# A retention layer and an MLP on one core: scores and sums of a head pair in one block of products, and a new order of the first units

## The chip, the cores and the metric

The kernel runs on one core of a Trainium2 chip. The time is the device time of one execution in microseconds (us); the kernel before took 1026.29 us (median of 3 runs, 1025.18 to 1026.33). Lower is better. "Faster" and "slower" mean a change of more than 2%.

The engines of the core work side by side, each through its own instructions in order: TensorE (PE in the profile, PEld for its weight loads) multiplies matrices and writes them to PSUM; VectorE (DVE), ScalarE (ACT) and GpSimd (POOL) work element by element; SyncE (SP) starts most of the transfers (DMA). An engine waits on semaphores where it needs another engine's result, or a buffer that another still reads.

## The reference

Per batch and head (8 batches, 8 heads, 576 positions, 64 features), a retention layer: causal scores with a decay that depends on the distance, times the values. Then an MLP with a PReLU over all 8 x 576 = 4608 tokens.

```python
# q, k, v: (8, 8, 576, 64)
scores = 64 ** -0.5 * np.matmul(q, k.transpose(0, 1, 3, 2))
gamma  = 1.0 - 2.0 ** (-5.0 - np.arange(8))
rel    = pos[:, None] - pos[None, :]
Dmat   = np.where(rel >= 0, gamma[:, None, None] ** rel, 0.0)
x      = np.matmul(scores * Dmat, v)            # -> (4608, 512): tokens x (head, feature)
h      = x @ w_in                               # w_in (512, 2048), 64-bit floats in memory
g      = np.maximum(h, 0) + alpha * np.minimum(h, 0)
out    = g @ w_out                              # w_out (2048, 512)
```

## The kernel before

Names used below. A *pair* n is two heads of one batch: 32 pairs, 4 to a batch. Its 576 positions are 9 chunks of 64. Within a chunk the kernel takes masked *scores* (tile `ps`, then `mt`); over the chunks it keeps *running sums* of k^T v (products in tile `pu`, sums in `su`, copied into `vn`); the *values* (`pv`) are then one product per chunk and head of [sums; v] with [q; scores], and land in x^T (`xb`). A *block* kb is 256 tokens; there are 18. A *unit* (kb, i) is one eighth of the MLP of a block. Blocks 0 and 1 are done in the plain way while the weights arrive and are converted; from block 2 on, both products of the MLP are done by a 7-product scheme (7 products of half-size matrices instead of 8), so a unit is 14 products `ph` of 128 columns, then sums on VectorE to `g`, then 7 products `po` of 256 columns. In the trace each f32 product shows as two matmul records.

One unit, and the sums at the end of a block:

```python
    def mlp_unit(kb, i):                       # ps_h has one buffer for each tag
        ph = [ps_h.tile([P, 4, P], FP32, tag=f"psh{m}") for m in range(2)]
        for n, (m, o, l, r) in enumerate((...)):          # 7 products, 2 parts each
            for cc in range(2):
                nc.tensor.matmul(ph[m][:, o], w_in[...], r[:, cc], ...)
        g = mlp.tile([P, 8, P], FP32, tag="g")
        nc.scalar.copy(g[:, 7], ph[0][:, 2])
        for o, x0, x1 in (...):                           # 4 sums that read ph (3 of 128x256)
            nc.vector.tensor_tensor(out=o, in0=x0, in1=x1, op=ALU.add)
        for m in range(2):
            nc.vector.tensor_scalar(g[...], g[...], 0.0, alpha[...], ALU.min, ALU.mult)
        nc.vector.scalar_tensor_tensor(...)               # max(x, 0) + the above, 128x512
        for o, x0, x1, op in (...):                       # 4 sums, 128x128
            ins = nc.vector.tensor_tensor(...)
        pend.append((kb, i, g))
        if len(pend) > 1:
            mlp_out()                          # the po of the unit BEFORE this one

    def mlp_out():
        kb, i, g = pend.pop(0)
        if i == 0:
            acc[kb] = [ps_o.tile([P, 2, HM], FP32, tag=f"pso{n}") for n in range(4)]  # 1 buffer
        for n, (x, y) in enumerate(PROD):      # 7 products into po0, po0, po1, po1, po2, po2, po3
            nc.tensor.matmul(acc[kb][n // 2][:, n % 2, :], g[:, x, :], w_out[i][:, y, :], ...)
        if i == NU - 1:
            out_block(kb, acc.pop(kb))

    def out_block(kb, po):                     # end of a block
        nc.scalar.copy(s1, p1)
        for o, x, y, op in (...):              # 6 sums 128x256 that read po0..po2
            nc.vector.tensor_tensor(out=o, in0=x, in1=y, op=op)
        nc.vector.tensor_tensor(out=osb[:, 1, 0], in0=p4, in1=u3, op=ALU.add)  # reads po3
```

A later pair (ps_a has two buffers for all its tiles, one PSUM bank each), and the loop that deals pairs and units:

```python
    def pair_scores(n, kT, qT):
        ps = [ps_tile([P, NM, C], ...) for p2 in range(2)]
        ...                                    # 9 chunks x 2 heads: 18 products 64x64
        for h2 in range(2):
            nc.scalar.copy(mt[half(h2), h2]..., qT[half(h2)])
        for p2 in range(2):
            for h2 in range(2):                # 4 masks, 64x320 and 64x256
                nc.vector.scalar_tensor_tensor(out=mt[...], in0=ps[p2][...], scalar=th[...],
                                               in1=mask[...], ...)
    def pair_states(n, kn, vn):
        ps = [ps_tile([P, NM - 1, D], f"pu{p2}_{n}") for p2 in range(2)]
        ...                                    # 8 chunks x 2 heads: 16 products 64x64
        nc.scalar.copy(su[:, 0::2], ps[0])
        ...                                    # VectorE: 2 of 64x256, 3 of 128x64, 1 of 128x192
    def pair_sums(vn, su):
        for h2 in range(2):
            nc.scalar.copy(vn[half(h2), h2, 1:], su[half(h2)])

    for n, (b, c) in enumerate(pairs):         # from pair 8 on
        ...
        share = -(-len(queue) // (NPAIR - c))  # 4 or 5 units to a pair
        cuts = [(share + i) // 3 for i in range(3)][::-1]
        kT, qT = turned.pop(n)
        mt = pair_scores(n, kT, qT)
        pop_units(cuts[0])
        pair_sums(vn, pair_states(n, kn, vn))
        pop_units(cuts[1])
        ... scale_pair(n + 1); transposes(n + 1)
        pair_values(n, vn, mt)
        pop_units(cuts[2])
```

The first batch is taken in parts of 256 positions, with all heads at once. The pieces of the weights are converted from 64-bit floats by `piece_in` (ScalarE, two operations) and `piece_out` (VectorE, three of 128x512, then one on GpSimd):

```python
    def part_states(x):
        ...                                    # 32 products
        for j in range(4):
            u = banks[j % 2][:, j // 2]
            if was is None:
                nc.scalar.copy(sums[x][j], u)
            else:
                nc.vector.tensor_tensor(out=sums[x][j], in0=was, in1=u, op=ALU.add)
            was = sums[x][j]
    def part_values(x):
        ...
        nc.scalar.copy(to[:, 0], banks[0])     # x^T for the first units
        for h2 in range(2):
            nc.scalar.copy(to[half(h2), 1], banks[1][half(1 - h2)])
    def plain_out(kb, i, g):
        for m in range(2):
            for x in range(2):
                nc.tensor.matmul(acc[kb][m], g[:, 2 * x + m], w_out[i][...], ...)
```

Of the kernel before, what the change touches and what calls it, by code (L numbers as in the profile page):

```python
# [18 lines left out]
def kernel(  # L19
# [54 lines left out]

    IN_FLIGHT = 5 << 18
    flight = []

    def load(to, src, size):
        ins = nc.sync.dma_start(to, src)
        if gated[0]:  # L80
            ahead = size
            for other, n in reversed(flight):
                if ahead >= IN_FLIGHT:
                    tc.add_manual_dep(ins.ins, other.ins.name, mybir.DependencyInfo(
                        mybir.DependencyClass.Sync, mybir.DependencyReason.DATA),
                        reason="bytes in flight")
                    break
                ahead += n
            flight.append((ins, size))

    gated = [True]

# [280 lines left out]

    def mlp_out():
        kb, i, g = pend.pop(0)
        if kb in PLAIN:
            return plain_out(kb, i, g)
        if i == 0:
            acc[kb] = [ps_o.tile([P, 2, HM], FP32, tag=f"pso{n}", name=f"po{n}_{kb}")
                       for n in range(4)]  # L380
        for n, (x, y) in enumerate(PROD):
            nc.tensor.matmul(acc[kb][n // 2][:, n % 2, :], g[:, x, :], w_out[i][:, y, :],  # L382
                             start=(i == 0 and n % 2 == 0),
                             stop=(i == NU - 1 and (n % 2 == 1 or n == 6)),
                             skip_group_check=True)
        if i == NU - 1:
            out_block(kb, acc.pop(kb))

    def plain_out(kb, i, g):
        if i == 0:
            acc[kb] = [ps_o.tile([P, DM], FP32, tag=f"pso{2 * kb + m}", name=f"po{m}_{kb}")
                       for m in range(2)]
        for m in range(2):
            for x in range(2):
                nc.tensor.matmul(acc[kb][m], g[:, 2 * x + m],  # L397
                                 w_out[i][:, 2 * x:2 * x + 2].rearrange("p x f -> p (x f)"),
                                 start=(i == 0 and x == 0), stop=(i == NU - 1 and x == 1))
        if i == NU - 1:  # L400
            po = acc.pop(kb)
            osb = ring.tile([P, 2, DM], FP32, tag=f"o{kb}", name=f"osb_{kb}")
            for m in range(2):
                t0 = kb * TB + m * P
                nc.scalar.copy(osb[:, m], po[m])
                nc.sync.dma_start(out[t0:t0 + P, :], osb[:, m])
        if kb == PLAIN[-1] and i % UST == UST - 1:
            waiting.extend((w_in[i // UST], x) for x in S_WORK)
            waiting.extend((w_out[j], x) for j in range(i + 1 - UST, i + 1) for x in T_WORK)
# [39 lines left out]

    def mlp_unit(kb, i):  # L450
        if kb not in xt:
# [5 lines left out]
        for n, (m, o, l, r) in enumerate((  # L457
# [3 lines left out]
            for cc in range(2):  # L461
                nc.tensor.matmul(ph[m][:, o], w_in[i // UST][:, l, i % UST, cc], r[:, cc],  # L462
                                 start=(n in (0, 3) and cc == 0), stop=(n in (2, 6) and cc == 1),
                                 skip_group_check=True)

# [19 lines left out]
        combine(3, ins)  # L486
        assert i < NU - UST or not waiting
        pend.append((kb, i, g))
        if len(pend) > 1:
# [14 lines left out]

    def pop_units(n):
        for _ in range(min(n, len(queue))):
            kb, i = queue.pop(0)
            mlp_unit(kb, i)
            if i == NU // 2 and kb + 1 < NKB and ready[kb + 1] <= done[0]:
# [54 lines left out]
    def pair_states(n, kn, vn):  # L564
        c = pairs[n][1]
        ps = [ps_tile([P, NM - 1, D], f"pu{p2}_{n}") for p2 in range(2)]
        for j in range(NJ - 1):
            for h2 in range(2):
                x = (h2, 1 - h2)[j % 2]
                nc.tensor.matmul(ps[j % 2][half(x), j // 2], kn[half(1 - h2), j],  # L570
                                 vn[half(1 - h2), h2, j], start=True, stop=True)
        su = attn.tile([P, S], FP32, tag="kT", name=f"su_{n}")[:, 0:S - D].rearrange(
            "p (j d) -> p j d", d=D)
        g1, g2 = gch[:, 0, c:c + 1], gch[:, 1, c:c + 1]
        nc.scalar.copy(su[:, 0::2], ps[0])
        for h2 in range(2):
            nc.vector.scalar_tensor_tensor(
                out=su[half(h2), 1::2], in0=su[half(h2), 0::2], scalar=g1[half(h2)],
                in1=ps[1][half(1 - h2)], op0=ALU.mult, op1=ALU.add)
        for j in range(3, NJ - 1, 2):  # L580
            nc.vector.scalar_tensor_tensor(out=su[:, j], in0=su[:, j - 2], scalar=g2,
                                           in1=su[:, j], op0=ALU.mult, op1=ALU.add)
        nc.vector.scalar_tensor_tensor(out=su[:, 2::2], in0=su[:, 1:NJ - 3:2], scalar=g1,  # L583
                                       in1=ps[0][:, 1:], op0=ALU.mult, op1=ALU.add)
        return su

    def pair_sums(vn, su):
        for h2 in range(2):
            nc.scalar.copy(vn[half(h2), h2, 1:], su[half(h2)])  # L589

    def pair_values(n, vn, mt):
# [80 lines left out]
    def part_states(x):  # L672
# [12 lines left out]
        for j in range(4):  # L685
            u = banks[j % 2][:, j // 2]
            if was is None:
                nc.scalar.copy(sums[x][j], u)
            else:
                nc.vector.tensor_tensor(out=sums[x][j], in0=was, in1=u, op=ALU.add)  # L690
# [6 lines left out]
    def part_values(x):  # L697
# [23 lines left out]
        to = xb[x].rearrange("p c (m q s) -> p q c m s", m=2, q=2)  # L721
        nc.scalar.copy(to[:, 0], banks[0])
        for h2 in range(2):
            nc.scalar.copy(to[half(h2), 1], banks[1][half(1 - h2)])  # L724

# [40 lines left out]
    fetch(6)  # L766
    load_part(1)
    fetch(8)
    load_part(2)
# [3 lines left out]
    part_scale(0, 2)  # L773
    part_scores(0)
    part_states(0)
    piece_in(2)
# [3 lines left out]
    aps = ps_a.tile([P, NFC], FP32, tag="psa", name="aps")  # L780
    nc.tensor.transpose(aps, a16, ident[0:NFC, 0:NFC])
    nc.vector.tensor_copy(alpha, aps)
    nc.vector.tensor_scalar(nalpha, alpha, -1.0, None, ALU.mult)
    piece_in(3)
    piece_out(2)
    part_scale(1, 1)
    piece_in(1)
    plain_unit(0, 0)
# [3 lines left out]
    part_transposes(1, 0)  # L792
    mlp_out()
    part_transposes(1, 1)
    piece_out(1)
    piece_in(1)
    piece_out(1)
    part_scores(1)
    part_states(1)
    part_scale(2, 1)  # L800
    part_scale(2, 2)
    piece_in(1)
    plain_unit(0, 1)
    piece_out(1)
    plain_relu()
    piece_in(1)
    part_values(1)
    part_carry(1)
    last_transposes()
# [17 lines left out]

    gated[0] = False

# [56 lines left out]
    for n, (b, c) in enumerate(pairs):  # L886
# [7 lines left out]
        share = -(-len(queue) // (NPAIR - c))  # L894
        cuts = [(share + i) // 3 for i in range(3)][::-1]
        kT, qT = turned.pop(n)
        mt = pair_scores(n, kT, qT)
        pop_units(cuts[0])
        pair_sums(vn, pair_states(n, kn, vn))
        pop_units(cuts[1])  # L900
        if n + 1 < len(pairs):
            scale_pair(n + 1)
            turned[n + 1] = transposes(n + 1)
        pair_values(n, vn, mt)
        del loaded[n]
        pop_units(cuts[2])
        if c == NPAIR - 1:
# [32 lines left out]
```

## Time and profile before

| | busy, us | share of the span |
|---|---|---|
| TensorE, products (PE) | 1007.9 | 98% |
| TensorE, weight loads (PEld) | 891.0 | 87% |
| VectorE (DVE) | 768.8 | 75% |
| ScalarE (ACT) | 267.5 | 26% |
| GpSimd (POOL) | 176.7 | 17% |

The span of the profiled execution is 1024.7 us. Up to some 160 us the plain units run; from there to the end the 7-product units, with pairs 8 to 31 between them up to some 880 us. A line of the timeline has: start in us, duration in us, engine, line of the kernel, operation, tile written <- tiles read, shapes, count; in brackets, idle time before it and what ended it. A duration there runs to the end of the last instruction and overlaps the next line, so the time that a piece costs its engine is best read from start to start.

### The profile page before, as it was taken

The page shows a single profiled execution, that of the slowest core. Times are in us where ns is not written, and L with a number is a line of the kernel's source. Part 1 is how long each engine was busy: PE and PEld are TensorE (multiplying, and loading weights), DVE is VectorE, ACT ScalarE, POOL GpSimd, SP SyncE. Part 2 cuts the span into 40 slices and gives each one's busy share as a digit, 9 for nine tenths or more (in the row PEclk, how much of TensorE's full clock was granted, in tenths as well). Part 3 has the DMA queues.
Part 4 walks back from the last instruction along what each step waited for, and adds up shares of the span by engine and source line. Part 5 has one row for each costly group of instructions (what it writes and reads, how often), then busy time and mean ns, then how long its engine had stood idle before and what let it go on. Part 6 is the DMA issues. An engine that isn't in the chain of part 4 may idle for free.

```text
span 1024.7 us, 23101 instructions
## 1 busy us (share of the span) xinstructions
PE 1007.9 (98%) x9385; PEld 891.0 (87%) x9385; DVE 768.8 (75%) x2041; ACT 267.5 (26%) x599; POOL 176.7 (17%) x198
## 2 busy tenths in 40 slices
PE   6899999999999999999999999999999999999998
PEld 5666668999999999999999999999999999999997
DVE  7669967777878787776868787877787776667665
ACT  4556652223222222022122222222222211000000
POOL 4656675200200010100010000200020001010000
PEclk9999999999999999999999999999999999999999
DMA  9975744223223222112113222222222100000000
GB/s 237 234 195 146 184 75 97 46 59 59 62 42 67 49 46 57 24 45 45 41 31 67 47 52 46 63 46 59 48 47 57 24 22 2 22 1 21 1 21 22
DMA packets 229308, 64.30 MB, mean 63 GB/s; under 512 B 214337, under 2 KB 222545, under 8 KB 229201
## 3 DMA queue, kind: packets, MB, share of 16 engines
q1 hardware_dynamic: 227088, 62.29, 26.8%
q8 instruction: 74, 1.21, 0.5%
q10 hardware_dynamic: 2112, 0.53, 0.3%
q14 instruction: 34, 0.27, 0.1%
HBM read 53.35 MB, written 9.44 MB: 61 GB/s over the span
## 4 chain that ended last, share of the span: by engine, by line
PE 97%; DVE 1%; DMA 1%; ACT 0%; issue 0%; POOL 0%; ACTq 0%; DVEq 0%; POOLq 0%
PE ph L462 40%; PE po L382 38%; PE po L397 6%; PE ph L418 5%; PE pv L600 3%; PE ps L551 2%; PE pu L570 2%; DMA w_out<-in_q_dram 1%; PE pv L717 0%; PE pv L706 0%; PE ps L660 0%; DVE w_out L690 0%; PE pt L641 0%; DVE wc L308 0%; DVE pa L667 0%
## 5 line engine op out<-in xcount | busy, mean ns | idle before, releaser
L382 PE MATMUL po<-w_out,g 128*128 128x256 f32 x1792 | 407.8, 379 | 0.0
L382 PEld LDWEIGHTS po<-w_out,g 128*128 128x128 f32 x1792 | 331.1, 190 | 39.4
L473 DVE TENSOR_TENSOR g<-ph,g 128x256 f32<-128x256 f32 (+1 forms) x512 | 187.5, 387 | 184.9 <-ACT g L468 112.7
L462 PE MATMUL ph<-xb,w_in 128*128 128x128 f32 x2048 | 277.8, 279 | 0.0
L462 PEld LDWEIGHTS ph<-xb,w_in 128*128 128x128 f32 x2048 | 253.2, 192 | 8.1 <-issue 0.5
L462 PE MATMUL ph<-xt,w_in 128*128 128x128 f32 x1536 | 213.4, 275 | 0.0
L462 PEld LDWEIGHTS ph<-xt,w_in 128*128 128x128 f32 x1536 | 192.1, 192 | 0.0
L468 ACT COPY g<-ph 128x128 f32<-128x128 f32 x128 | 33.9, 265 | 395.7 <-PE ph L462 375.6
L484 DVE TENSOR_TENSOR g<-g 128x128 f32<-128x128 f32 x512 | 126.8, 289 | 7.8
L478 DVE SCALAR_TENSOR_TENSOR g<-g 128x512 f32<-128x512 f32 x128 | 91.7, 717 | 3.9
L476 DVE TENSOR_SCALAR g<-g,alpha 128x256 f32<-128x256 f32 x256 | 85.0, 374 | 3.7
L523 POOL TENSOR_TENSOR qx<-qx,tabx 128x576 f32<-128x576 f32 x28 | 32.7, 1167 | 310.9 <-DMA qx<-in_q_dram 255.0
L418 PE MATMUL ph<-xb,w_in 128*128 128x256 f32 x256 | 60.2, 390 | 1.4 <-ACT xb L724 1.4
L559 DVE SCALAR_TENSOR_TENSOR mt<-ps,th,mask 64x320 f32<-64x320 f32 (+1 forms) x112 | 57.8, 516 | 4.5 <-PE ps L551 2.7
L397 PE MATMUL po<-w_out,g 128*128 128x512 f32 x128 | 58.5, 599 | 0.9 <-DVE g L434 0.9
L418 PEld LDWEIGHTS ph<-xb,w_in 128*128 128x128 f32 x256 | 49.1, 195 | 11.1 <-issue 2.4
L448 POOL TENSOR_TENSOR xt<-xb 128x256 f32<-128x256 f32 x16 | 11.6, 726 | 214.4 <-PE ph L462 202.1
L448 POOL TENSOR_TENSOR xt<-xb,xt 128x256 f32<-128x256 f32 x32 | 23.6, 738 | 142.4 <-ACT xb L609 141.7
L528 ACT ACTIVATE vn<-vn,tabv 64x576 f32<-64x576 f32 x56 | 43.3, 773 | 16.2 <-DMA vn<-in_v_dram 15.7
L397 PEld LDWEIGHTS po<-w_out,g 128*128 128x128 f32 x128 | 23.5, 190 | 24.9 <-issue 22.5
L589 ACT COPY vn<-su 64x512 f32<-64x512 f32 x56 | 34.5, 616 | 37.5 <-DVE su L583 36.8
L609 ACT COPY xb<-pv 128x256 f32<-128x256 f32 (+3 forms) x84 | 22.6, 321 | 79.1 <-PE pv L600 79.1
(120 smaller groups left out, 687.0 us busy)
## 6 DMA issues: line engine op xcount, KB each, us to landing
out_dram<-osb SPq DMA_DIRECT2D x36, 256.0 KB, 2.3
kx<-in_k_dram SPq DMA_DIRECT2D x112, 72.0 KB, 2.8
qx<-in_q_dram SPq DMA_DIRECT2D x112, 72.0 KB, 2.5
vn<-in_v_dram SPq DMA_DIRECT2D x56, 144.0 KB, 3.2
kn<-in_k_dram SPq DMA_DIRECT2D x56, 144.0 KB, 3.2
raw<-in_moe_w_in_dram SPq DMA_DIRECT2D x24, 256.0 KB, 4.4
raw<-in_moe_w_out_dram SPq DMA_DIRECT2D x10, 512.0 KB, 4.3
w_in<-in_moe_w_out_dram SPq DMA_DIRECT2D x6, 512.0 KB, 5.4
```

The costliest lines, as they stand in the source:

```text
L382: nc.tensor.matmul(acc[kb][n // 2][:, n % 2, :], g[:, x, :], w_out[i][:, y, :], start=(i == 0 and n % 2 == 0), stop=(i == NU - 1 and (n % ...
L397: nc.tensor.matmul(acc[kb][m], g[:, 2 * x + m], w_out[i][:, 2 * x:2 * x + 2].rearrange("p x f -> p (x f)"), start=(i == 0 and x == 0), sto ...
L418: nc.tensor.matmul(ph[:, x], w_in[i // UST][:, cc // 2 * 2 + x, i % UST, cc % 2], xb[kb][:, cc], start=(cc == 0 and x == 0), stop=(cc == N ...
L448: nc.gpsimd.tensor_tensor(out=o, in0=x0, in1=x1, op=ALU.subtract)
L462: nc.tensor.matmul(ph[m][:, o], w_in[i // UST][:, l, i % UST, cc], r[:, cc], start=(n in (0, 3) and cc == 0), stop=(n in (2, 6) and cc == ...
L473: nc.vector.tensor_tensor(out=o, in0=x0, in1=x1, op=ALU.add)
L476: nc.vector.tensor_scalar(g[:, 4 + 2 * m:6 + 2 * m], g[:, 2 * m:2 * m + 2], 0.0, alpha[:, fc:fc + 1], ALU.min, ALU.mult)
L478: nc.vector.scalar_tensor_tensor(out=g[:, 0:4].rearrange("p x t -> p (x t)"), in0=g[:, 0:4].rearrange("p x t -> p (x t)"), scalar=0.0, in1 ...
L484: ins = nc.vector.tensor_tensor(out=g[:, o, :], in0=g[:, x0, :], in1=g[:, x1, :], op=op)
L528: nc.scalar.activation(vn[x, h2], vn[x, h2], ACTF.Copy, scale=tabv[x, c:c + 1])
L559: nc.vector.scalar_tensor_tensor(out=mt[to, h2, p2::2], in0=ps[p2][half(x), 0:nm], scalar=th[to, 3, h:h + 1], in1=mask[to, None, :].to_bro ...
L589: nc.scalar.copy(vn[half(h2), h2, 1:], su[half(h2)])
```

## The change

It has two parts. For the later pairs (8 to 31), the products of the scores and those of the running sums stand in one block on TensorE, inside a unit, between its `ph` products and the `po` products of the unit before; so TensorE changes between 128x128 and 64x64 products twice per pair instead of three times. Two PSUM banks hold both kinds (8 chunks of scores and 8 of sums fill them); the ninth chunk's scores go into the unused quarter of the unit's own `ph` bank. The work of VectorE and ScalarE on these products follows that of the unit. For the first units, the order is new: running sums of the first part by ScalarE and GpSimd instead of VectorE, x^T in two halves so that the first products can start after the first, `plain_out` by halves of `g` with the transposes of part 1 between them, more bytes of loads in flight, and pieces of weights taken in at other places.

```diff
+    in_flight[0] = 7 << 18            # after load_part(1); 5 << 18 until then
...
-    def plain_out(kb, i, g):
+    def plain_out(kb, i, g, between):
-        for m in range(2):
-            for x in range(2):
+        for x in range(2):
+            if x and between:
+                between()
+            for m in range(2):
                 nc.tensor.matmul(acc[kb][m], g[:, 2 * x + m], ...)
...
-    def mlp_unit(kb, i):
+    def mlp_unit(kb, i, front=None):
...                                    # after the products ph of the unit:
+        rest = front(ph[0][:, 3]) if front else None
...                                    # after all that VectorE does for g:
+        if rest:
+            rest()
         pend.append((kb, i, g))
         if len(pend) > 1:
             mlp_out()
...
+    def pair_front(n, kT, qT, kn, vn):
+        def products(extra):
+            ps = [ps_tile([P, 2, NM - 1, C], f"ps{p2}_{n}") for p2 in range(2)]
+            for j in (NJ - 1, *range(NJ - 1)):
+                for h2 in range(2):
+                    x = half((1 - h2, h2)[j % 2])
+                    nc.tensor.matmul(extra[x, 0:C] if j == NJ - 1 else ps[j % 2][x, 0, j // 2],
+                                     kT[half(h2), chunk(j)], qT[half(h2), chunk(j)], ...)
+            for j in range(NJ - 1):
+                for h2 in range(2):
+                    x = half((h2, 1 - h2)[j % 2])
+                    nc.tensor.matmul(ps[j % 2][x, 1, j // 2], kn[half(1 - h2), j],
+                                     vn[half(1 - h2), h2, j], ...)
+            for h2 in range(2):
+                to = half(1 - h2)
+                nc.vector.scalar_tensor_tensor(              # 64x64
+                    out=mt[to, h2, NJ - 1], in0=extra[to, 0:C], ...)
+            def rest():
+                for h2 in range(2):
+                    nc.scalar.copy(mt[half(h2), h2]..., qT[half(h2)])
+                for p2 in range(2):
+                    for h2 in range(2):                      # four of 64x256
+                        nc.vector.scalar_tensor_tensor(out=mt[...], in0=ps[p2][half(x), 0], ...)
+                pair_sums(vn, running_sums(n, ps[0][:, 1], ps[1][:, 1]))
+            return rest
+        return products
...
     def part_states(x):
-            if was is None:
+            if x == 0:
                 nc.scalar.copy(sums[x][j], u)
+                if j:
+                    nc.gpsimd.tensor_tensor(out=sums[x][j], in0=was, in1=sums[x][j], op=ALU.add)
...
     def part_values(x):
-        nc.scalar.copy(to[:, 0], banks[0])
-        for h2 in range(2):
-            nc.scalar.copy(to[half(h2), 1], banks[1][half(1 - h2)])
+        for c in (slice(0, 2), slice(2, 4)) if x == 0 else (slice(0, NPAIR),):
+            nc.scalar.copy(to[:, 0, c], banks[0][:, c])
+            for h2 in range(2):
+                nc.scalar.copy(to[half(h2), 1, c], banks[1][half(1 - h2), c])
...                                    # start: pieces earlier, part_scale(2, .) later
     part_scores(0)
+    piece_in(1)
     part_states(0)
...
-    mlp_out()
-    part_transposes(1, 1)
+    mlp_out(lambda: part_transposes(1, 1))
...
     for n, (b, c) in enumerate(pairs):
-        cuts = [(share + i) // 3 for i in range(3)][::-1]
-        kT, qT = turned.pop(n)
-        mt = pair_scores(n, kT, qT)
-        pop_units(cuts[0])
-        pair_sums(vn, pair_states(n, kn, vn))
-        pop_units(cuts[1])
+        pop_units(1, pair_front(n, *turned.pop(n), kn, vn))
+        pop_units(share // 2)
         if n + 1 < len(pairs):
             scale_pair(n + 1)
             turned[n + 1] = transposes(n + 1)
-        pair_values(n, vn, mt)
+        pair_values(n, vn, mts.pop(n))
-        pop_units(cuts[2])
+        pop_units(share - 1 - share // 2)
```

## The prediction

> **What bounds the kernel now.** I read the chain of waits first: it says which engine has to be relieved.
>
> ```profile
> PE 97%; DVE 1%; DMA 1%; ACT 0%; issue 0%; POOL 0%; ACTq 0%; DVEq 0%; POOLq 0%
> ```
>
> TensorE carries 97% of the chain, so from the first products on the time is its work plus its gaps. Second, the waits of TensorE, which are the gaps:
>
> ```profile
> PE pv L717 <- issue: 1.8, 1, 1.8
> PE ph L418 <- ACT xb L724: 1.4, 1, 1.4
> PE po L397 <- DVE g L434: 0.9, 1, 0.9
> PE pv L706 <- POOL w_out L670: 0.9, 1, 0.9
> ```
>
> With 6 us at the very start for k, and four below 0.4 us, that is all: every gap lies in the first 42 us, none in the long part. Third, TensorE's timeline in the long part, read from start to start:
>
> ```profile
> 500.26 3.19 PE L382 MATMUL po<-w_out,g 128*128 128x256 f32 x14
> 503.28 1.05 PE L462 MATMUL ph<-xb,w_in 128*128 128x128 f32 x8
> ...
> 506.41 3.19 PE L382 MATMUL po<-w_out,g 128*128 128x256 f32 x14
> 509.53 0.69 PE L570 MATMUL pu<-vn,kn 64*64 64x64 f32 x32
> 510.15 1.16 PE L462 MATMUL ph<-xb,w_in 128*128 128x128 f32 x8
> ...
> 513.38 3.19 PE L382 MATMUL po<-w_out,g 128*128 128x256 f32 x14
> ...
> 533.22 3.19 PE L382 MATMUL po<-w_out,g 128*128 128x256 f32 x14
> ...
> 536.34 0.80 PE L551 MATMUL ps<-qT,kT 64*64 64x64 f32 x36
> 537.07 1.16 PE L462 MATMUL ph<-xb,w_in 128*128 128x128 f32 x8
> ...
> 540.29 3.19 PE L382 MATMUL po<-w_out,g 128*128 128x256 f32 x14
> ```
>
> A bare unit takes 506.41 - 500.26 = 6.15 us, 3.02 of it po and 3.13 ph. With the sums' products it takes 6.97, with the scores' 7.07: 0.82 and 0.92 more. The blocks themselves last 0.62 and 0.73 start to start, so about 0.2 us each is the change of size: po before the block takes 3.12 instead of 3.02, and the first eight ph after it about 0.1 more too. Fourth, VectorE's timeline at the end of a block, because VectorE at 75% is the next engine:
>
> ```profile
> 592.58 2.11 DVE L559 SCALAR_TENSOR_TENSOR mt<-ps,th,mask 64x256 f32<-64x256 f32 x4 [0.17 <-PE ps L551]
> 594.72 0.42 DVE L473 TENSOR_TENSOR g<-ph,g 128x256 f32<-128x256 f32 x1
> ...
> 600.35 0.42 DVE L368 TENSOR_TENSOR osb<-po,u 128x256 f32<-128x256 f32 x1
> 600.68 0.42 DVE L368 TENSOR_TENSOR osb<-po,s 128x256 f32<-128x256 f32 x1
> 601.01 0.42 DVE L369 TENSOR_TENSOR osb<-po,u 128x256 f32<-128x256 f32 x1
> ...
> 606.17 0.98 DVE L577 SCALAR_TENSOR_TENSOR su<-su,gch,pu 64x256 f32<-64x256 f32 x2 [0.54 <-ACT su L575]
> ```
>
> The reader should see that the work lies in portions: masks of the scores at 592.58, the end of the block until 601.3, the running sums at 606.17, a unit apart from each other. From 592.58 to 601.34 VectorE hardly rests, and TensorE does not wait. That spacing is what the change gives up.
>
> **What the skill says.** "Perfetto Trace Analysis", Identifying the Most-Contended Engine: matmul busy time is no measure of how near TensorE is to its limit. The trace agrees: PE is shown 98% busy although the same unit takes 6.15 or 7.07 us; so I count start to start. "VectorE: DVE Perf Modes", Two Vector instructions with no wait between them: an instruction whose input or output starts in another group of 32 partitions than the last one's waits until the earlier ones have finished, otherwise it may start sooner. The trace fits: the four masks on 64 partitions take 2.14 us start to start, not less than their summed durations, while the sums at a block's end follow each other every 0.33 us at 0.42 us each. So I take the half-partition operations at full length. "TensorE: Matmul & The Clock Gate", What's actually happening: a gate halves the clock after an idle window of about 3.4 us that runs freely. The trace shows a granted clock of 0.50 between 20 and 22 us, after the gaps of 1.8 and 1.4 us; shorter gaps need not remove it. "PSUM — Partial Sum Buffer", The four PSUM rules: GpSimd can't reach PSUM, hence ScalarE's copies ahead of GpSimd's sums in the new start; no run here shows it.
>
> **The change, part by part.**
>
> (a) Products in one block. One change of size less for each of the pairs 8 to 31: 24 x 0.2 = 4.8 us less. The number of products stays the same (18 + 16 per pair).
>
> (b) VectorE gets masks and sums in one portion. I took the order in which the built program puts its instructions. In the steady rhythm most fronts (as I call the units that hold a pair's block) are the units 4 and 0 of a block: nine pairs (12, 14, 16, 20, 22, 24, 26, 28, 30) fall on unit 0, one unit after the last of a block. There VectorE must do, ahead of the end of the block, all of the front's work. Time t from the start of the first ph of unit 0, taking pair 12 and block 4. TensorE, if nothing holds it: ph to 3.1; scores and sums 0.73 + 0.62 + 0.2 at the ends, to 4.6; po of block 3's last unit to 7.6; ph of unit 1 to 10.7; po of unit 0 from 10.7 to 13.7, where po0, po1, po2 begin at 10.7, 11.6 and 12.4. VectorE: it starts with the two 64x64 masks, which wait for the block's first products, at 3.35, and then follows its order. Lengths from the timelines: 0.28 each for the small masks (an estimate: a 64x256 mask takes 0.48, less 192 columns at the rate between 64x256 and 64x320 masks, 0.48 and 0.55); 0.33 for a 128x256 sum, 0.20 for one of 128x128; a transpose 0.69; 0.55 for the two scalings and 0.60 for the large operation of g; 0.48 for a mask of 64x256 and for each of the two half-partition running sums; 0.20 for a chained sum.
>
> Two small masks 0.6 (to 3.95); sum, transpose, sum 1.35 (5.3); mask, two sums, mask 1.5 (6.8); scalings, mask 1.0 (7.8); large operation, mask 1.1 (8.9); three sums of g, running sum, sum, running sum 1.75 (10.65); first sum of the block's end (11.0: po0 free); two chained sums and the second and third of the block's end 1.05 (12.05: po1 free); the rest of the running sums 0.55 (12.6); three sums that read po2 1.0 (13.6: po2 free). Meanwhile ScalarE copies the running sums from 12.7, two of 0.63, to 13.95.
>
> TensorE then: po0 at 11.1 instead of 10.7; po1 at 12.15; after it the program has placed six values products of pair 12, before po2, and these need ScalarE's copies: 14.05, done 14.35; then po2 and po3, 1.3, to 15.65 instead of 13.7. Of these 1.9 us, 0.4 come back since the six products are done, and one more change of size costs 0.2: 1.7 us per pair, 9 x 1.7 = 15.3 us more. The lag does not go further: the sums of ph of unit 1 run from 13.9 on, the bank of ph0 is free at 14.3 and wanted at 15.65.
>
> At the other fronts, without a block's end, the same count gives running sums done at 11.6 and g of the next unit's last ph read at about 13, with the bank wanted at 13.7: no wait.
>
> (c) The first units. x^T in halves: three copies of 256 columns (0.37 by the same operation elsewhere) instead of three of 512 (1.75 together), so the first ph starts 0.65 us sooner. The transposes of part 1 between the halves of plain_out hide 0.3 us of a wait for ScalarE; scaling of the last part moved behind lets the masks of part 1 on GpSimd be in time: 0.9. Three sums, together 1.33 us, leave VectorE, so that the second piece of w_in, which ended on GpSimd at 20.9, ends about 1.4 earlier. The clock of one half cost 5.28 - 3.72 = 1.56 us in the first unit; I give half of that a chance: 0.8. Together 2.7 us less. It carries through, since nothing after 58 us waits.
>
> Sum: 1026.3 - 4.8 + 15.3 - 2.7 = 1034.1; I say 1033, a little toward the next rival.
>
> **The rivals.** First: VectorE keeps up, and the change brings what it seems to be for, 4.8 + 2.7 less: 1019. For it speaks that VectorE is busy only 75% of the time and never held TensorE before; against it, that a share of the span is no measure of a portion: between 3.35 and 12.4 there are 9.05 us, and 10.25 us of work that stands ahead of po2. Second: the portion is a wait at every front, if the masks start later than I think or are held longer by the changes of partition group, or if GpSimd slows VectorE at unit 4 (its sums of x^T come there; beside them two scalings took 1.34 us at 534.5 instead of 0.62). Then 15 more fronts lose up to 1 us and the nine up to 3: some 1053. Third: only the early order counts: more bytes in flight could delay the loads wanted first (DMA is at 0.97 to 1.2 of its engines up to 40 us), and a second front of waits on weights would cost 2 to 4 us instead of giving 2.7: about 1038.
>
> **Range and chances.** The loss at block ends is a small difference of two large sums (10.25 against 9.05, and ScalarE's copies behind it): an error of 10% in VectorE's lengths moves it by 1 us per pair, 9 us in all. So 1019 to 1046 should hold it 8 times in 10. Faster by over 2% would be under 1005.8, more than all gaps and changes of size together: 0.01. Slower by over 2% is over 1046.8: 0.09. Within 2%: 0.90.
>
> **What would show it.** Right: waits of TensorE for VectorE (the block's end) at po and for ScalarE (copies of the running sums) at the values products, near the start of blocks 4, 5, 6 and 9 to 14, some 1.5 to 2 us each, and none near the starts of blocks 7 and 8; units with a front at about 6.15 + 1.55 us. Wrong in (b): po of unit 0 in those blocks runs its 3.02 us after ph without a gap. Wrong in (a): a front costs 1.7 us or more over a bare unit. Wrong in (c): the first ph later than 19.0 us, or the unit at 46.7 us no earlier than before.

## The result and the profile after

The changed kernel takes 1051.66 us (median of 6 runs, 1049.01 to 1053.72) against 1026.84 us before (6 runs, 1025.18 to 1027.75): ratio 1.0241, 95% interval 1.0224 to 1.0259. It is slower by over 2%, and outside the predicted range of 1019 to 1046; it is near the size that the second rival gave (1053). The chain of waits of the changed kernel, in shares of the span, stood at PE 97% before:

```profile
PE 85%; DVE 11%; ACT 2%; issue 1%; DMA 1%; SPq 0%; DVEq 0%; ACTq 0%
```

VectorE now carries 11% of the chain. Where, say the waits of TensorE (waiting for; us in total, times, longest one):

```profile
PE po L381 <- DVE osb L367: 11.5, 9, 1.3
...
PE po L381 <- DVE u L367: 4.2, 7, 0.8
PE pv L773 <- issue: 2.4, 1, 2.4
PE pv L654 <- ACT vn L597: 1.7, 8, 0.3
PE ph L463 <- DVE g L476: 1.0, 1, 1.0
```

The three lines on `osb`, `u` and `vn` did not exist before. Nine times TensorE waits at `po` for the first sum of a block's end (`osb`), seven times more, right behind, for a later one (`u`), and eight times at the values products for ScalarE's copies (`vn`). Nine is the number of pairs whose front lies on unit 0 of a block; of the eight waits for `vn`, seven lie there (none in blocks 5 and 9) and one behind pair 11. The last line is one single wait in block 2. TensorE's timeline at the first of the nine, pair 12 at the start of block 4 (start, duration, engine, line, operation, shapes, count; in brackets the wait before it):

```profile
265.48 1.05 PE L463 MATMUL ph<-xb,w_in 128*128 128x128 f32 x8
...
268.16 0.61 PE L463 MATMUL ph<-xt,w_in 128*128 128x128 f32 x4
268.70 0.27 PE L612 MATMUL ph<-qT,kT 64*64 64x64 f32 x2
...
269.90 3.29 PE L381 MATMUL po<-w_out,g 128*128 128x256 f32 x14
273.02 1.05 PE L463 MATMUL ph<-xb,w_in 128*128 128x128 f32 x8
...
275.70 0.61 PE L463 MATMUL ph<-xt,w_in 128*128 128x128 f32 x4
277.58 1.10 PE L381 MATMUL po<-w_out,g 128*128 128x256 f32 x4 [1.27 <-DVE osb L367]
279.29 1.13 PE L381 MATMUL po<-w_out,g 128*128 128x256 f32 x4 [0.60 <-DVE u L367]
280.35 0.61 PE L654 MATMUL pv<-mt,vn 128*64 128x64 f32 x8
281.15 0.34 PE L654 MATMUL pv<-mt,vn 128*64 128x64 f32 x4 [0.19 <-ACT vn L597]
281.42 1.56 PE L381 MATMUL po<-w_out,g 128*128 128x256 f32 x6
282.82 1.05 PE L463 MATMUL ph<-xb,w_in 128*128 128x128 f32 x8
```

The unit with the front takes 273.02 - 265.48 = 7.54 us, and the block of both kinds 269.90 - 268.70 = 1.20 us (0.73 + 0.62 apart, before). The next unit stalls at po0, at po1 and at the values, in the order that the prediction gave. It lasts 282.82 - 273.02 = 9.80 us; the same unit before, with one block of small products in it, took 279.10 - 272.23 = 6.87:

```profile
272.23 1.05 PE L462 MATMUL ph<-xb,w_in 128*128 128x128 f32 x8
...
278.47 0.69 PE L570 MATMUL pu<-vn,kn 64*64 64x64 f32 x32
279.10 1.16 PE L462 MATMUL ph<-xb,w_in 128*128 128x128 f32 x8
```

The idle times in brackets are less than what a wait costs, since they count from the end of the last product, which overlaps the next start: po0 starts 277.58 - 275.70 = 1.88 us after the last four records of `ph`, where it was 275.36 - 274.91 = 0.45 before, so it comes 1.43 us late with 1.27 in the bracket. VectorE's timeline of the same stretch:

```profile
269.08 0.58 DVE L623 SCALAR_TENSOR_TENSOR mt<-ph,th,mask 64x64 f32<-64x64 f32 x2 [1.44 <-PE ph L612]
270.05 0.42 DVE L476 TENSOR_TENSOR g<-ph,g 128x256 f32<-128x256 f32 x1 [0.39 <-ACT g L471]
...
277.01 0.42 DVE L367 TENSOR_TENSOR osb<-po,s 128x256 f32<-128x256 f32 x1
277.35 1.02 DVE L589 SCALAR_TENSOR_TENSOR su<-su,gch 128x64 f32<-128x64 f32 x1
278.30 0.41 DVE L367 TENSOR_TENSOR s<-po,s 128x256 f32<-128x256 f32 x1
278.63 0.27 DVE L589 SCALAR_TENSOR_TENSOR su<-su,gch 128x64 f32<-128x64 f32 x1
```

and those of ScalarE and GpSimd:

```profile
269.75 0.27 ACT L471 COPY g<-ph 128x128 f32<-128x128 f32 x1 [5.51 <-DVE mt L623]
277.15 1.15 POOL L528 TENSOR_TENSOR qx<-qx,tabx 128x576 f32<-128x576 f32 x1 [11.44 <-DVE su L585]
```

Two things in them were not in the prediction. ScalarE's copy of `ph`, which the first sum of `g` needs, stands still until VectorE's small masks are done, although the copied product is the first of the unit's seven: masks and copy then follow each other. And one chained sum of 128x64 takes 1.02 us instead of 0.27 while GpSimd scales q of the next pair. In the kernel before, GpSimd scaled q as well, but after 178 us none of these chained sums took longer than 0.29 us: the new order is what put the two side by side.

Unit by unit against before: the first 7-product unit starts 1.03 us earlier (152.76 instead of 153.79). A pair without a block's end gains 0.26 us net. The nine steps from the start of unit 1 to that of unit 2 in blocks 4, 5, 6 and 9 to 14 grow by 2.93, 4.27, 2.95, 3.98, 2.82, 2.19, 2.95, 2.81 and 2.18 us: 27.1 together, against 27.3 for everything after 152.76. What lies outside these steps nearly cancels: small gains at the other fronts against small losses, the largest of them 1.5 us in block 2, where the single wait is. From now on I call what follows the first 7-product unit the *loop*: 870.91 us before, 898.24 after.

### The profile page after: what moved, and what is told of

Read it like the earlier page. It is cut to its first block, busy times and chain, and to the rows that moved or that the text cites. A ratio compares the mean times of both kernels' runs of the same rounds, so it can differ in the third digit from the quotient of the medians. Undisturbed runs are those within 1.5% of the kernel's fastest.

```text
span 1051.0 us, 23057 instructions
## 1 busy us (share of the span) xinstructions
PE 1016.6 (97%) x9385; PEld 899.9 (86%) x9385; DVE 779.8 (74%) x2086; ACT 269.2 (26%) x605; POOL 178.7 (17%) x201
## 3 DMA queue, kind: packets, MB, share of 16 engines
q8 instruction: 74, 1.21, 0.5%
## 4 chain that ended last, share of the span: by engine, by line
PE 85%; DVE 11%; ACT 2%; issue 1%; DMA 1%; SPq 0%; DVEq 0%; ACTq 0%
PE ph L463 35%; PE po L381 33%; PE ph L419 6%; PE po L398 5%; PE pv L654 3%; DVE mt L634 2%; DVE su L589 1%; DVE g L476 1%; ACT vn L597 1%; DVE su L585 1%; DVE g L487 1%; DVE qT L539 1%; DVE g L481 1%; PE ps L612 1%; PE ps L618 1%
## 5 line engine op out<-in xcount | busy, mean ns | idle before, releaser
L381 PE MATMUL po<-w_out,g 128*128 128x256 f32 x1792 | 418.8, 384 | 15.8 <-DVE osb L367 11.5
L381 PEld LDWEIGHTS po<-w_out,g 128*128 128x128 f32 x1792 | 330.3, 191 | 63.4 <-issue 12.9
L463 PE MATMUL ph<-xb,w_in 128*128 128x128 f32 x2048 | 272.7, 276 | 0.0
L463 PEld LDWEIGHTS ph<-xb,w_in 128*128 128x128 f32 x2048 | 257.1, 192 | 7.9 <-issue 0.7
L487 DVE TENSOR_TENSOR g<-g 128x128 f32<-128x128 f32 x512 | 130.2, 295 | 6.5
L623 DVE SCALAR_TENSOR_TENSOR mt<-ph,th,mask 64x64 f32<-64x64 f32 x48 | 13.6, 283 | 61.5 <-PE ph L612 61.2
L419 PEld LDWEIGHTS ph<-xb,w_in 128*128 128x128 f32 x256 | 49.3, 196 | 10.7 <-issue 2.4
L654 PEld LDWEIGHTS pv<-mt,vn 128*64 128x64 f32 x1008 | 36.3, 139 | 16.7 <-issue 12.2
L634 DVE SCALAR_TENSOR_TENSOR mt<-ps,th,mask 64x256 f32<-64x256 f32 x96 | 46.1, 480 | 2.3
```

The source lines that it names most:

```text
L419: nc.tensor.matmul(ph[:, x], w_in[i // UST][:, cc // 2 * 2 + x, i % UST, cc % 2], xb[kb][:, cc], start=(cc == 0 and x == 0), stop=(cc == N ...
L487: ins = nc.vector.tensor_tensor(out=g[:, o, :], in0=g[:, x0, :], in1=g[:, x1, :], op=op)
L634: nc.vector.scalar_tensor_tensor(out=mt[to, h2, p2:NJ - 1:2], in0=ps[p2][half(x), 0], scalar=th[to, 3, h:h + 1], in1=mask[to, None, :].to_ ...
L654: nc.tensor.matmul(pv[j >= j1][half(h2), j - (j1 if j >= j1 else 0)], vn[:, h2, j], mt[:, h2, j], start=True, stop=True)
```

## The experiments

The theory after the result: the nine block ends lose more than their working, because the masks start late, because ScalarE's copy hangs on them, and because GpSimd holds VectorE up. The rivals: the new start costs time that only shows later; the lag lies in the amount of VectorE's work, not its place; GpSimd has no part in it. All ratios are against the kernel before.

**The new start alone.** The start of the changed kernel with the loop of the kernel before:

```diff
-        pop_units(1, pair_front(n, *turned.pop(n), kn, vn))
-        pop_units(share // 2)
+        cuts = [(share + i) // 3 for i in range(3)][::-1]
+        kT, qT = turned.pop(n)
+        mts[n] = pair_scores(n, kT, qT)
+        pop_units(cuts[0])
+        pair_sums(vn, pair_states(n, kn, vn))
+        pop_units(cuts[1])
```

> Only the new order of the first units; the loop of the later pairs is that of before. Theory (the loss lies at the nine block ends): 1.0 us less than before, as the unit after plain unit (1,0) starts 1.04 us earlier in the trace of the change (57.54 against 58.58), so about 1025.8 and a ratio of 0.999. Rival (the early order is a part of the loss, by delayed loads): longer than before by some us, 1029 or more.

Measured: 1025.86 us, ratio 0.9991 (0.9976 to 1.0006). In the trace the first 7-product unit is 0.92 us earlier than before (152.87) and the loop takes 871.13 us, as before. So the new start is no loss; a gain of 1 us fits, but the interval does not exclude none. The 27 us come from the pairs alone.

**The front later, by one unit.** Pairs with four or five units take one of them ahead of the front, so that no front lies on unit 0:

```diff
+        lead = int(share >= 4)
+        pop_units(lead)
         pop_units(1, pair_front(n, *turned.pop(n), kn, vn))
-        pop_units(share // 2)
+        pop_units(share - 2 - lead)
         ...                                # next pair's scaling and transposes, values
-        pop_units(share - 1 - share // 2)
+        pop_units(1)
```

> The change, but with one more unit ahead of each pair's front where a pair has four or more, so that fronts fall on units 1 and 5 and no longer on unit 0. Theory (VectorE's portion stands ahead of the sums of a block's end): no waits of TensorE for VectorE at po, the 30 us of the nine fronts are gone, and what stays is 24 pairs x 0.27 us and 1.0 us at the start: 1026.8 - 7.5 = 1019. Rival (the portion is too much for the unit behind any front that comes close to a block's end, wherever it stands): the waits move with the front, at least half of the loss stays, 1035 or more.

Measured: 1041.76 us, ratio 1.0154 (1.0134 to 1.0173): a miss of over 20 us. The waits for the block's end are gone, but the waits of TensorE show another in their place:

```profile
PE pv L654 <- ACT vn L597: 15.2, 31, 1.0
```

and TensorE's timeline behind the front of pair 12, whose block of small products started at 275.31, shows why:

```profile
282.76 3.19 PE L381 MATMUL po<-w_out,g 128*128 128x256 f32 x14
285.88 0.34 PE L654 MATMUL pv<-mt,vn 128*64 128x64 f32 x4
287.08 0.33 PE L654 MATMUL pv<-mt,vn 128*64 128x64 f32 x2 [0.87 <-ACT vn L597]
287.72 1.15 PE L654 MATMUL pv<-mt,vn 128*64 128x64 f32 x30 [0.31 <-ACT vn L597]
```

One unit lies between front and values. The running sums come after all of VectorE's work for the front's unit, and ScalarE copies them only then: the values arrive first. I had freed the block's end and taken away the distance that hid the rest of the same chain.

**q scaled by ScalarE instead of GpSimd**, with the order of the changed kernel:

```diff
-        nc.gpsimd.tensor_tensor(out=qh, in0=qh, in1=tabx[...].to_broadcast(...), op=ALU.mult)
+        if n > 8:                          # else as before
+            for x in range(2):
+                nc.scalar.activation(qh[:, :, x], qh[:, :, x], ACTF.Copy,
+                                     scale=tabx[:, c, x:x + 1])
```

> The change, but q of the next pair is scaled by ScalarE instead of GpSimd. Theory (in seven of the nine fronts GpSimd's scaling holds up one chained sum on VectorE by about 0.75 us, and TensorE waits for it): the sum takes 0.28 us everywhere, the steps at these fronts fall from 2.8 to 4.3 us towards 2.1, some 6 us less than the change in all: 1045 to 1046. Rival (the order of the instructions alone sets the wait, GpSimd only fills idle time): within 1 us of the change, 1051.

Measured: 1043.52 us, ratio 1.0162 (1.0145 to 1.0179), 8 us less than the changed kernel. VectorE's timeline at the same place of block 4:

```profile
276.75 0.42 DVE L367 TENSOR_TENSOR osb<-po,s 128x256 f32<-128x256 f32 x1
277.10 0.28 DVE L594 SCALAR_TENSOR_TENSOR su<-su,gch 128x64 f32<-128x64 f32 x1
277.29 0.42 DVE L367 TENSOR_TENSOR s<-po,s 128x256 f32<-128x256 f32 x1
```

The chained sum is back at 0.28 us. All nine steps now grow by 2.18 to 2.19 us, which is what blocks 11 and 14 showed in the changed kernel. The waits of TensorE keep their first line:

```profile
PE po L381 <- DVE osb L367: 11.5, 9, 1.3
```

The wait at po0 is the same to the tenth; the one for `u` behind it has gone. GpSimd's part is real, and it is not the larger part.

**The portion behind po.** The masks and running sums come after `mlp_out`, so after the block's end:

```diff
-        if rest:
-            rest()
         pend.append((kb, i, g))
         if len(pend) > 1:
             mlp_out()
+        if rest:
+            rest()
```

> The change, but the masks and running sums of a front are put into the program behind the po products of the unit before, so behind the sums of a block's end. Theory: po no longer waits for the block's end on VectorE; the same work then delays the sums that free the next unit's ph banks, by 1 to 1.5 us in each of the nine fronts: 1030 to 1036. Rival (it is ScalarE's copies of the running sums, needed by the values products in the middle of po, that hold TensorE): they come later still, no gain, 1050 or more.

Measured: 1034.40 us, ratio 1.0073 (1.0058 to 1.0088). The waits at `po` for the block's end are gone; in the waits of TensorE

```profile
PE ph L463 <- DVE g L476: 4.0, 10, 1.0
```

shows the next: VectorE is now late with the sums that free a bank of `ph`. A change of order inside the portion moves the wait, and takes away over half of the loss: this loop lasts 879.59 us.

**The front one unit later, the values further off.** As the second experiment, but the values stay where they have two or three units between (the fourth pair of a batch, after which the next batch is queued, keeps its front first):

```diff
+        tail = int(c == NPAIR - 1)
+        lead = 1 - tail
+        pop_units(lead)
         pop_units(1, pair_front(n, *turned.pop(n), kn, vn))
-        pop_units(share // 2)
+        pop_units(share - 1 - lead - tail)
         ...                                # next pair's scaling and transposes, values
-        pop_units(share - 1 - share // 2)
+        pop_units(tail)
```

> The change with fronts moved off unit 0 as in the second run, but with two units or more between a front and its values products (the last pair of a batch keeps the place it had). Theory (block ends cost the change its 30 us, and the second run lost its gain to values products that came one unit too soon for ScalarE's copies): no waits at po, and none of 1 us at the values products; 24 pairs x 0.25 us and 1 us at the start are left: 1027.2 - 7 = 1020. Rival (blocks of both kinds of products always leave a wait of about 0.7 us somewhere behind them): 1027 or more.

Measured: 1020.88 us, ratio 0.9938 (0.9925 to 0.9952): below the kernel before, clear of noise, but by less than the 2% that count as faster here. In the loop the largest wait of TensorE is a single one of 0.3 us:

```profile
PE pv L654 <- ACT vn L597: 0.3, 1, 0.3
```

Same products, same VectorE operations, same start as in the changed kernel: 31 us less by place alone. This refutes the rival of the amount of work.

**The same, and q scaled by ScalarE.**

> The run above, with q scaled by ScalarE. Theory: GpSimd's hold-ups cost nothing where no block end waits behind them: the same time as the run above within 1 us. Rival (hold-ups cost at every front): 3 us or more less than the run above.

Measured: 1017.14 us, ratio 0.9905 (0.9891 to 0.9918), 3.7 us less than the run before it: the rival's number. The loops take 867.13 and 863.82 us, so 3.3 of it lie there. What VectorE does in the loop, in one window each (window, its length, then busy us and count of PE, PEld, DVE, ACT, POOL, clock, DMA), first with GpSimd scaling:

```profile
155.00:1020.00 865.00, 859.70 (x7868) 796.65 (x7867) 663.71 (x1854) 176.85 (x427) 80.93 (x96) 1.00 0.20 42
```

then with ScalarE scaling:

```profile
155.00:1015.00 860.00, 854.82 (x7852) 793.81 (x7850) 644.80 (x1854) 194.92 (x470) 52.01 (x70) 1.00 0.20 42
```

The same 1854 operations of VectorE last some 19 us less when GpSimd does not scale. Of that only 3.3 us reach the end. They do so in small steps: from unit to unit, 14 steps of TensorE are 0.06 to 0.48 us longer with GpSimd scaling, 3.5 us together, and 12 of them hold the values of a pair. The waits of the weight loads show a part of it; with GpSimd scaling

```profile
PEld po L381 <- DVE g L481: 1.8, 8, 0.3
```

and with ScalarE scaling

```profile
PEld po L381 <- DVE g L481: 0.3, 1, 0.3
```

so units can start late with hardly a wait of PE to be seen.

**The small masks behind the sums of g.** On top of the third experiment (ScalarE scaling, order of the changed kernel), the two 64x64 masks come after the four sums that read `ph`:

```diff
-        rest = front(ph[0][:, 3]) if front else None
+        last_chunk, rest = front(ph[0][:, 3]) if front else (None, None)
         ...                                # copy of ph by ScalarE, four sums that read ph
+        if last_chunk:
+            last_chunk()                   # the two 64x64 masks
```

> The change with q scaled by ScalarE, and the two small masks of the ninth chunk behind the four sums that read ph instead of ahead of them. Theory (the small masks start VectorE's work late: its first sum of g waits for the block's products, and ScalarE's copy of ph waits for the masks, 0.25 + 0.4 us and the sum's own 0.33): each of the nine steps falls by 0.9 us, 1043.5 - 8 = 1035. Rival (ScalarE's copies of the running sums, at the end of the chain, or the order of the instructions set the wait): less than 2 us gained, 1042 or more.

Measured: 1037.30 us, ratio 1.0101 (1.0088 to 1.0115), 6.2 us less than the third experiment, where the theory said 8. ScalarE's and VectorE's timelines:

```profile
267.12 0.27 ACT L471 COPY g<-ph 128x128 f32<-128x128 f32 x1 [4.91 <-PE ph L619]
```

```profile
267.42 0.42 DVE L476 TENSOR_TENSOR g<-ph,g 128x256 f32<-128x256 f32 x1 [1.79 <-ACT g L471]
```

The copy now waits for TensorE alone, and the first sum of `g` starts 3.89 us after unit 0's first `ph` (263.53) instead of 4.57. The wait at po0 falls by almost half:

```profile
PE po L381 <- DVE osb L367: 6.2, 9, 0.7
```

That is 5.3 of the 6.2 us. The program also put the values products elsewhere here (two of pair 12's records ahead of po2, sixteen into the `ph` of the next unit), so the last 0.9 can't be given to the copy alone. Nor is the copy's wait parted here from the masks' own: both went with this edit.

**The small masks late, in the best order.**

> Fronts moved off the block ends, q scaled by ScalarE, and the small masks behind the sums that read ph. Theory: no wait of TensorE is left in the units after the plain stage, so a further relief of VectorE brings nothing: within 1 us of the run without the last edit, 1017. Rival (VectorE's late start costs something at every front): 3 us or more less, 1014.

Measured: 1018.47 us, ratio 0.9913 (0.9900 to 0.9926). No more than without it: where the portion is out of the way, 0.6 us inside it are worth nothing.

**The best order with the start of before.** The pairs of the best version, the first units of the kernel before:

```diff
-            if x == 0:
+            if was is None:
                 nc.scalar.copy(sums[x][j], u)
-                if j:
-                    nc.gpsimd.tensor_tensor(out=sums[x][j], in0=was, in1=sums[x][j], op=ALU.add)
...                                # likewise x^T whole, plain_out, bytes in flight, pieces
```

> The later pairs as in the run with fronts off the block ends and q scaled by ScalarE, the first units in the order of before. Theory (the new order of the first units is worth about 1 us, the later pairs about 6 to 7): 1 us slower than with the new start, 1019 to 1020. Rival (the new start is worth nothing by itself, its gain in the trace was the state of TensorE's clock in that execution): equal within 0.5 us to the run with the new start.

Measured: 1020.06 us, ratio 0.9931 (0.9919 to 0.9943).

**The best version again, beside it:**

> The run with fronts off the block ends and q scaled by ScalarE once more, beside the other two: 1017, within 1.5 us. If chance in the first units made its first result, 1019 or more.

Measured: 1017.71 us, ratio 0.9912 (0.9899 to 0.9926). The start is worth 2.3 us here by the medians, where the first experiment showed 1.4 (1027.23 against 1025.86); in the traces the first 7-product unit comes at 155.23 and 152.65, and both loops last the same, 863.57 and 863.75. This version, with the front one unit later, the values far behind and q scaled by ScalarE, takes 0.9% less than the kernel before, and by the medians 3.2% less than the changed one (1017.71 and 1051.66). Its chain of waits, in the profile of its first measurement:

```profile
PE 95%; DVE 2%; DMA 1%; issue 1%; ACT 1%; SPq 0%; DVEq 0%; ACTq 0%; POOL 0%; POOLq 0%
```

TensorE carries the end again.

## Why the prediction was wrong

**The bound, and the place of the loss: right.** The waits came in the nine pairs named, at the blocks named, none at blocks 7 and 8, at po0, po1 and the values in the order worked out. VectorE's spacing is what the change gave up; moving the front by one unit, with the values kept further off, brings it back.

**Step (b), the size: this is the step that failed.** It said 1.7 us per pair, 15.3 in all. Measured against the best order, which has no such waits, the loop lost 898.24 - 863.82 = 34.4 us; 1.6 of them lie ahead of block 4, which leaves 32.9 us, 3.7 for each of the nine pairs. The prediction's clock for pair 12, beside the traces (us after unit 0's first `ph`):

| | predicted | changed kernel | ScalarE scales q |
|---|---|---|---|
| small masks start | 3.35 | 3.60 | |
| first sum of g starts | 3.95 | 4.57 | |
| first sum of the block's end starts | 10.65 | 11.53 | 11.53 |
| po0 starts | 11.1 | 12.10 | 12.11 |
| po2 starts | 14.35 | 15.94 | 15.19 |
| ph of unit 2 starts | 15.65 | 17.34 | 16.59 |

Four terms were missing or short. The masks wait for all four records of the ninth chunk, which end 0.25 later than I had put them. The first sum follows the masks not at once but behind ScalarE's copy, which waits for them: 0.37 more (4.57 - 3.95 - 0.25). The list from there to the block's end was 0.26 short (6.96 instead of 6.70), and po0 starts 0.57 after the first of those sums, not 0.45: 0.12. That makes the whole 1.0 us at po0. Then GpSimd: 0.75 us between po0 and the end, gone when ScalarE scales. I had seen GpSimd slow VectorE, but at unit 4 and as part of a rival, and had left it out of the sum at unit 0, where q of the next pair is scaled.

From block 4 on, the same in shares per pair, all against the best order: the changed kernel 3.7; without GpSimd's scaling (24.3 us in all) 2.7; with the small masks late besides (18.8 us) 2.1. So GpSimd costs 1.0, the masks' place with ScalarE's copy 0.6, and 0.4 is left over the predicted 1.7, which start, list and po0's release make up roughly. GpSimd's 1.0 is more than the 0.75 of pair 12, although two of the nine pairs (blocks 11 and 14) are not held up at all: some 1 us lies outside the nine steps, and 2.3 us come with a lower clock. Behind the waits in blocks 5 and 9, TensorE's granted clock (second number from the end but one) fell:

```profile
337.00:343.00 6.00, 5.16 (x28) 4.02 (x28) 5.20 (x16) 1.23 (x2) 0.00 (x0) 0.72 0.40 114
560.00:566.00 6.00, 6.00 (x36) 4.85 (x37) 4.25 (x13) 1.23 (x2) 0.00 (x0) 0.72 0.48 127
```

Those two steps grew by 4.27 and 3.98 instead of some 2.95: 2.3 us more for both, spent on slow products behind the waits (1.27 and 0.84 us in block 5, 1.27 and 0.54 in block 9). In the profile with ScalarE scaling, where the second wait is gone, it does not happen: its nine steps are alike. That is one execution of each kernel; that the waits are the cause fits, and is not shown.

The estimate "an error of 10% in VectorE's lengths moves it by 1 us per pair" was the right warning, drawn too small: the list of lengths was short by 4% only (6.70 for 6.96), and what waits for what between the engines did the rest.

**Step (a): right, a little low.** A front costs 7.54 - 6.15 = 1.39 us; before, the two blocks cost 0.92 + 0.82 = 1.74. Net of the values, a pair without a block's end gains 0.26 us, and the loop of the best order is 7.1 us shorter than before, 0.3 per pair; 0.2 was predicted.

**Step (c): right in direction, 1.0 us in the trace instead of 2.7.** Its sign of being wrong came: the first plain `ph` starts at 20.01, later than the 19.0 named and than the 19.67 before. The three waits named did shrink or go: from the transpose ahead of it (`aps`) to the first plain `ph` it takes 1.00 us instead of 1.61, and the waits of 0.3 and 0.9 us are no longer there. Against that stand two losses, seen in TensorE's timeline of the changed kernel (before: 16.93, 1.21 and [1.78]; 19.67, 5.28):

```profile
17.20 1.88 PE L773 MATMUL pv<-pT,w_out 64*32 64x64 f32 x82 [2.39 <-issue]
...
20.01 5.72 PE L419 MATMUL ph<-xb,w_in 128*128 128x256 f32 x16 [0.72 <-ACT xb L781]
```

A wait of "issue" became 0.6 us longer, and the clock fell behind it, already in the 82 records; these (1.81 us start to start instead of 1.13) and the first `ph` (0.44 longer) cost 1.1 us more, so the 0.8 us that I gave to a better clock became a loss. In the profile of the best version that clock stayed at full:

```profile
20.00:25.00 5.00, 4.31 (x22) 3.10 (x21) 3.94 (x9) 4.34 (x9) 3.05 (x3) 1.00 0.82 182
```

its "issue" waits there were of 1.4 us, and its first 7-product unit came at 151.58; the same kernel run again had a wait of 2.37 us and half a clock, and 152.65. Over the ten profiles with the new start, the first 7-product unit comes between 151.20 and 154.01, so one execution can't size this term. Why "issue" takes longer or shorter I did not find out.

**The rivals.** The first (VectorE keeps up, 1019) is what the best order makes of the same operations: 1017 to 1021. The second named both GpSimd and later masks, and its 3 us for each of the nine pairs was near the 3.7 measured; but it also had up to 1 us at each of 15 other fronts, and the waits did not spread there. That its total of 1053 came so near 1051.66 is luck in part. The third fell: the new start alone is no loss (1025.86 us).

**What the Trainium skill said.** "SBUF — State Buffer", Who interferes with whom: VectorE with two inputs in SBUF and a GpSimd operation that reads SBUF block each other for whole instructions, and the one that starts first goes on. The trace agrees: GpSimd's scaling runs from 277.15 to 278.30, and the chained sum (two inputs in `su`) that starts at 277.35 ends at 278.37; the sum before it, with one input in PSUM, ran into the same time at its usual 0.42. Had I laid the scaling into the prediction's list by this, 0.75 us for each pair where the two meet would have been in the sum. "TensorE: Matmul & The Clock Gate", What's actually happening, speaks of an idle window of about 3.4 us; here two waits of 1.27 and 0.54 us with 1.1 us of products between them, in block 9, were followed by half clock; in block 6 nearly the same two (1.27 and 0.63) were not.

## What to carry to other kernels

When a change gathers work into portions, lay each portion on the timeline of the engine that does it, with the engines that it waits for and the ones that can block it, and ask what stands next in that engine's order: here it was the end of a block, nine times, and one unit's shift, with the distance to the values kept, turned 2.4% more time than before into 0.6% less. Count the chain behind the portion too (running sums, copies, values): the distance taken away at its other end cost 21 us in the first attempt (1041.76 against 1020.88). An operation of another engine that is free on paper may sit on the one small operation that everybody waits for.

## What the runs showed of the hardware

- A GpSimd multiplication of 128x576 (1.15 us) held a VectorE operation of 128x64 with both inputs in SBUF to 1.02 us instead of 0.27; over the loop the same 1854 VectorE operations lasted some 19 us longer with such multiplications.
- Waits of TensorE of no more than 1.3 us each, two close together, were followed by half clock in two of seven cases of one execution (a granted clock of 0.72 over 6 us), and those two steps were another 1.0 and 1.3 us longer.
- Two kinds of 64x64 products in one block, 68 records, take 1.20 us, apart 0.73 + 0.62; with its changes of size, a front costs 1.39 us instead of the 1.74 of the two blocks before.
- A ScalarE copy of one part of `ph` did not start until VectorE's masks of another part of the same PSUM tile were done (VectorE then idled for 0.39 us). Moving the masks behind the sums gained 0.6 us per pair where the portion was on the path, and nothing where it was not.
